# A fused attention and two-MoE kernel: result tiles stored one batch at a time, and the side work of the first expert respread

## The chip, the cores and the metric

The kernel runs on 1 core of one Trainium2 chip. The metric is device time in microseconds (us) of one execution. Before the change it is 998.13 us (median of 3 runs, 998.01 to 1000.34). Engines are called as in the profile: PE is TensorE (PEld its weight loads), DVE VectorE, ACT ScalarE, POOL GpSimd, SP the engine that issues the transfers.

## The reference, cut to what matters

```python
x = attention(q, k, v)              # 4 x 8 heads, 576 rows of 64, window 128 -> x: 2304 x 512
x = moe(x, phi, w1, w2)             # soft slots; its result is c @ slot_out, 32 slots

def _moe2_ref(x, w_gate, w1, w2):   # N = 2304, D = 512, E = 8, F = 1024
    logits = x @ w_gate
    logits = logits - logits.max()
    P = np.exp(logits)
    for _ in range(8):
        P /= P.sum(1, keepdims=True) + 1e-09
        P /= P.sum(0, keepdims=True) + 1e-09
        P *= N / E
    out = np.zeros((N, D))
    for e in range(E):
        h = np.maximum(x @ w1[e], 0.0)
        out += P[:, e:e + 1] * (h @ w2[e])
    return out
```

The change touches the second MoE only: the eight normalising rounds on P, the preparation of an expert's weights, and the store of `out`.

## The kernel before, in words

**Stages.** Attention comes first; the first MoE's own products (L775, L849) run from 165.5 to 202.4 us of the span, and from the first `emit_z` at 210.9 us to the end the second MoE does its eight experts. The rest is about this last stage.

**The main loop.** The 2304 rows are 18 tiles of 128 rows; tile t holds 64 rows of batch 2bp and the same 64 rows of batch 2bp + 1, with `bp, c = divmod(t, 9)`. The loop is over m = 0 to 71, and m is expert e = m // 9 and n = m % 9: one m does the two tiles n and n + 9. The hidden layer h is made by `emit_z` (L967, twice for one m, 4 matmuls each) from the factored first MoE (`ct`) and the expert's `stk`; the second product is a Strassen-like scheme of 7 block products, each of 12 matmuls in halves of f16 (`prod`, L1039). So one m has 7 steps k_ = 0 to 6, and in step k_ the program issues, in this order: `emit_z` (k_ 0 and 1, for m + 1), `step` (the product of the step on PE and the `add` of an earlier product to `acc`), at k_ = 0 also `last(m - 1)` and `left(m, 7)`, then **one step of the side work** (`next(side, None)`), then `left(m + 1, k_)`, which makes one piece of the next m's left operands: on ACT (L977, L988, L996), DVE (L980, L992) and POOL (L999). The order within an engine is the order of the program; every engine works through its own list in order and waits where an operand is missing.

**The adds.** In the first expert (e = 0) the first add of a block is a copy on ACT (L1049), the others are adds on DVE (L1051); from e = 1 on all are DVE operations that multiply by the gate's column `pe_[e]` (L1053). PE overwrites a product's PSUM buffer only when the add has read it.

**The side work** is a chain of generators, each `yield` one step. For the next expert: `prep_w1` (32 matmuls L676, a maximum, scales, the copy of `stk`), a load of weights, `prep_w2a` and another load. `prep_w2a` first takes the magnitudes of the second weight matrix, 8 passes on ACT (L564), then their maximum, a power-of-two scale, and then in 44 steps turns the matrix into the seven f16 block operands `w2h` and `w2l`: casts on ACT (L637), scalings on ACT (L645), differences on POOL (L634). In the first expert there is more: `gate` (logits and exp of P) comes first in 6 steps, then `sinkhorn`, the eight rounds on P, stepped together with the preparation of expert 1 by `par`, one step of each for each step of the loop. A round has three steps: (A) five DVE operations L923 to L928 on P, (B) a matmul L930 that sums over partitions, (C) four DVE operations L933 to L936. What is left of the side work at n = 8, k_ = 2 is issued there in one go ("the drain").

**The stores.** In the last expert a tile is complete after its last add, and `store` (L1060 to L1064) issues one transfer for it on SP's queue: 128 rows of 512 f32, 256 KB, as 2 batches x 64 rows x 512; the very last tiles go in two halves of columns.

Of the kernel before, what the change touches and what calls it, by code (L numbers as in the profile page):

```python
# [12 lines left out]
ALU = mybir.AluOpType  # L13
# [11 lines left out]
def tile_kernel(ctx: ExitStack, tc: tile.TileContext, q, k, v, phi, w1, w2, w_gate, m1, m2, rel, out):  # L25
    nc = tc.nc
    B, H, S, D = q.shape
    N, DM = out.shape
    E, _, F = w1.shape
    NS = phi.shape[1]  # L30
    CH = 64
# [63 lines left out]
    with tc.manual_schedule():  # L95
        with ExitStack() as ab:
# [5 lines left out]
            with ExitStack() as at:  # L102
# [369 lines left out]
                side = []  # L472
# [12 lines left out]
                s = 0  # L485
                while s < NST + 4 or side or px:
                    t, hf = divmod(s, 2)
# [28 lines left out]
                    if s < NST and hf == 0:  # L516
                        bp, c = divmod(t, NCH)
# [27 lines left out]
            stk = {}  # L545
            w2c = {}
            wsum = {}

            def spread(am):

                dg = mp.tile([128, 128], F32, tag="sl", name="dg", bufs=1)
                nc.vector.tensor_scalar_mul(dg, idn, am)
                return dg
# [1 line left out]
            def largest(dg, ps):  # L555
                nc.tensor.matmul(ps, lhsT=ones, rhs=dg, start=True, stop=True)

            def prep_w2a(e, place):
                wsum[e] = mp.tile([128, 4, 256], F32, tag="t1", name="t1", bufs=1)

                am = mp.tile([128, 1], F32, tag="am2", name="am2")
                amp = mp.tile([128, FC], F32, tag="amp", name="amp")
                for i in range(FC):
                    nc.scalar.activation(out=wsum[e][:, 0:2].rearrange("p a b -> p (a b)"),  # L564
                                         in_=wt["m2", e][:, DM * i:DM * (i + 1)], func=AF.Abs, accum_out=amp[:, i:i + 1])
                    yield
                yield
                nc.vector.tensor_reduce(out=am, in_=amp, axis=AX.X, op=ALU.max)
                dg = spread(am)
                yield  # L570
                ps = place()
                largest(dg, ps)
# [146 lines left out]
            with ExitStack() as bs:  # L719
# [75 lines left out]
                for i in range(4):  # L795
                    for cp in range(4):
                        dst = selh if cp < 2 else sell
                        nc.vector.tensor_copy(out=dst[32 * i:32 * i + 32, 32 * cp:32 * cp + 32],
                                              in_=idn[32 * i:32 * i + 32, 32 * i:32 * i + 32])
# [79 lines left out]
            with ExitStack() as ms:  # L879
                ap_ = ms.enter_context(tc.tile_pool(name="acc", bufs=1, reuse_waits="tile"))  # L880
                acc = ap_.tile([128, NT, DM], F32, name="acc")
# [7 lines left out]
                def gate():  # L889

                    st4 = sp.tile([128, DC, 4, NS], F32, name="st4")
                    sgb = sp.tile([128, 4, E], F32, name="sgb")
                    nc.gpsimd.memset(sgb, 0.0)
                    nc.vector.tensor_copy(out=st4, in_=st.unsqueeze(2).to_broadcast([128, DC, 4, NS]))
                    yield
                    ps = pmt
                    for dc in range(DC):
                        nc.tensor.matmul(ps[:, 0:E], lhsT=st4[:, dc].rearrange("p a b -> p (a b)"),
                                         rhs=wg_sb[:, dc, :], start=(dc == 0), stop=(dc == DC - 1))
                    for i in range(4):  # L900
                        nc.scalar.copy(out=sgb[32 * i:32 * i + 32, i, :], in_=ps[32 * i:32 * i + 32, 0:E])
                    yield
                    yield
                    for g in range(NG):
                        nc.tensor.matmul(ps[:, 32 * g:32 * g + 32], lhsT=cTf[:, g, :],
                                         rhs=sgb.rearrange("p a b -> p (a b)"), start=True, stop=True)
                    l2 = ps[:, 0:NT * E]
                    mx = mp.tile([128, 1], F32, tag="mx", name="mx")
                    mg = mp.tile([128, 1], F32, tag="mg", name="mg")
                    nc.vector.tensor_reduce(out=mx, in_=l2, axis=AX.X, op=ALU.max)  # L910
                    dg = spread(mx)
                    yield
                    largest(dg, ps[:, 256:384])
                    yield
                    nc.vector.tensor_reduce(out=mg, in_=ps[:, 256:384], axis=AX.X, op=ALU.max, negate=True)
                    nc.scalar.activation(out=prob.rearrange("p a b -> p (a b)"), in_=l2, func=AF.Exp, bias=mg)
                    yield

                def sinkhorn():
                    sums_ = pmt[:, 384:384 + E]  # L920
                    for _ in range(8):
                        rs_ = mp.tile([128, NT], F32, tag="rs", name="rs")
                        nc.vector.tensor_reduce(out=rs_, in_=prob, axis=AX.X, op=ALU.add)  # L923
                        nc.vector.tensor_scalar_add(rs_, rs_, 1e-9)
                        nc.vector.reciprocal(rs_, rs_)
                        nc.vector.tensor_tensor(out=prob, in0=prob, in1=rs_.to_broadcast([128, NT, E]), op=ALU.mult)
                        c1 = mp.tile([128, E], F32, tag="c1", name="c1")
                        nc.vector.tensor_reduce(out=c1, in_=prob.rearrange("p t e -> p e t"), axis=AX.X, op=ALU.add)  # L928
                        yield
                        nc.tensor.matmul(sums_, lhsT=ones, rhs=c1, start=True, stop=True)  # L930
                        yield
                        c2 = mp.tile([128, E], F32, tag="c2", name="c2")
                        nc.vector.tensor_scalar_add(c2, sums_, 1e-9)  # L933
                        nc.vector.reciprocal(c2, c2)
                        nc.vector.tensor_scalar_mul(c2, c2, float(N) / E)
                        nc.vector.tensor_tensor(out=prob, in0=prob,  # L936
                                                in1=c2.unsqueeze(1).to_broadcast([128, NT, E]), op=ALU.mult)
                        yield
# [3 lines left out]
                def scale_p(e):  # L942
                    pe_[e] = mp.tile([128, NT], F32, tag="pe", name="pe", bufs=3)
                    nc.vector.tensor_scalar(out=pe_[e], in0=prob[:, :, e], scalar1=inv_s[:, e:e + 1],
                                            scalar2=inv_w[:, e:e + 1], op0=ALU.mult, op1=ALU.mult)
                    yield
# [4 lines left out]
                NP = NT // 2  # L951
# [107 lines left out]

                def store(t, c0=0, c1=DM):  # L1060
                    bp, c = divmod(t, NCH)
                    nc.sync.dma_start(
                        out=out.rearrange("(b s) d -> b s d", s=S)[2 * bp:2 * bp + 2, CH * c:CH * c + CH, c0:c1],
                        in_=acc[:, t, c0:c1])  # L1064

                NM = E * NP

# [44 lines left out]
                def chain(*gens):  # L1112
                    for g_ in gens:
                        yield from g_

                def par(x_, y_):

                    live = [x_, y_]
                    while live:
                        for g_ in list(live):  # L1120
                            if next(g_, 0) == 0:
                                live.remove(g_)
                        yield

                def loads(e, nm):
# [26 lines left out]
                for m in range(NM):  # L1152
                    e, n = divmod(m, NP)
                    if n == 0:
                        side = []
                        if e + 1 < E:
                            side = [prep_w1(e + 1), loads(e + 2, "m1"), prep_w2a(e + 1, lambda: pmt[:, 256:384]), loads(e + 2, "m2")]
                        if e == 0:
                            side = [gate(), par(chain(sinkhorn(), scale_p(0)), chain(*side))]
                        if e + 1 < E:  # L1160
                            side.append(scale_p(e + 1))
                        side = chain(*side)
                    for k_ in range(7):
                        if m and k_ < 2 and m + 1 < NM:
                            emit_z(m + 1, k_)
                        if m or k_ > 3:
                            step(m, k_)
                        elif k_ == 0:

                            step(m, 0)  # L1170
                            emit_z(m + 1, 0)
                            step(m, 1)
                            step(m, 2)
                        elif k_ == 1:
                            emit_z(m + 1, 1)
                            for kk_, nm in ((KS1, "s1"), (KS4, "s4")):
                                hi_s(0, kk_, nm)
                                lo_s(0, kk_, nm)
                            step(m, 3)
                        if k_ == 0:  # L1180
                            if m:
                                last(m - 1)
                            left(m, 7)
                        next(side, None)
                        if k_ in (4, 5) and NP - 1 <= m < 2 * NP - 1:
                            weigh((m + 1) % NP + NP * (k_ - 4))
                        if m + 1 < NM:
                            left(m + 1, k_)
                        if n == NP - 1 and k_ == 2:
                            for _ in side:  # L1190
                                pass
                last(NM - 1)
# [37 lines left out]
```

## Time and profile before

| | before |
|---|---|
| median of 3 runs | 998.13 us |
| profiled execution: its time | 1000.32 us |
| profiled execution: its span (first to last instruction) | 998.5 us |
| PE busy | 954.0 us, 96% |
| DVE busy | 746.4 us, 75% |
| ACT busy | 625.3 us, 63% |
| POOL busy | 574.9 us, 58% |
| mean granted clock of PE | 0.985 |

How to read it: the span is that of the profiled execution; its time has 1.8 us more around it. Busy time is an average over stages with different limits, so the shares of the whole span don't tell what bounds one stage; the rows below are therefore taken by stretches. A granted clock of 1.00 is 2.4 GHz, 0.50 is 1.2 GHz. A busy PE is not PE at its peak, as matmuls are pipelined.

### The profile page before, as it was taken

How to read it: one execution, taken by the hardware profiler on the slowest of the kernel's cores; microseconds unless marked ns; L12 is line 12 of the kernel's file. 1: busy time of each engine (PE TensorE's matmuls, PEld its weight loads, DVE VectorE, ACT ScalarE, POOL GpSimd, SP SyncE). 2: the span in 40 equal slices, each digit the busy share in tenths (PEclk: the TensorE clock that was granted, in tenths of full speed). 3: DMA queues.
4: the chain of work that ended last, by engine and by line, in shares of the span. 5: the costliest groups of instructions: out<-in, count | busy, mean ns of one | idle time of the engine just before them, and what ended most of it. 6: DMA issues, size and time to landing. Idle time of an engine off the chain costs nothing.

```text
span 998.5 us, 24140 instructions
## 1 busy us (share of the span) xinstructions
PE 954.0 (96%) x9341; PEld 815.9 (82%) x9341; DVE 746.4 (75%) x1932; ACT 625.3 (63%) x1529; POOL 574.9 (58%) x685
## 2 busy tenths in 40 slices
PE   8999999888899899999999999999999999999993
PEld 7887886356778788888888888888888888888883
DVE  6888895768965587777778777777787777777771
ACT  6878884734667577756656664766566656564540
POOL 2322211213389568947884896589569947884440
PEclk9999999999999999999999999999999999999997
DMA  8999998950200220041022002200220020001111
GB/s 180 251 237 215 249 278 297 386 200 13 84 1 1 94 88 1 2 136 46 2 80 101 2 2 88 93 2 2 94 88 1 2 95 2 2 1 40 53 52 48
DMA packets 93927, 90.07 MB, mean 90 GB/s; under 512 B 63094, under 2 KB 67062, under 8 KB 93814
## 3 DMA queue, kind: packets, MB, share of 16 engines
q1 hardware_dynamic: 93814, 88.54, 29.6%
q8 instruction: 73, 1.20, 0.5%
q14 instruction: 40, 0.33, 0.1%
HBM read 81.97 MB, written 4.72 MB: 87 GB/s over the span
## 4 chain that ended last, share of the span: by engine, by line
PE 85%; DVE 10%; ACT 2%; issue 1%; POOL 1%; DVEq 0%; POOLq 0%; ACTq 0%
PE x L1039 36%; PE y L1039 26%; PE z L967 6%; PE xp L276 4%; PE s L202 3%; PE pt L251 2%; PE pt L155 2%; PE m L676 2%; PE b L775 1%; DVE et L221 1%; DVE et L240 1%; DVE ops L980 1%; PE s L849 1%; PE pt L290 1%; PE warm L83 1%
## 5 line engine op out<-in xcount | busy, mean ns | idle before, releaser
L1039 PEld LDWEIGHTS <-ops 128*128 128x128 f16 x6048 | 595.1, 98 | 82.4 <-issue 9.8
L999 POOL TENSOR_TENSOR ops<-s,ops 128x512 f16<-128x512 f32 x287 | 331.7, 1159 | 236.2 <-ACT ops L996 198.7
L1039 PE MATMUL x<-w2h,ops 128*128 128x256 f16 x2304 | 418.5, 275 | 7.1 <-ACT acc L1049 3.2
L1039 PE MATMUL y<-w2h,ops 128*128 128x256 f16 x1728 | 319.5, 273 | 1.6 <-DVE acc L1051 1.6
L1039 PE MATMUL x<-w2l,ops 128*128 128x256 f16 x1152 | 316.4, 275 | 0.0
L996 ACT CAST ops<-s 128x512 f16<-128x512 f32 x288 | 177.7, 618 | 213.3 <-DVE s L992 210.9
L1039 PE MATMUL y<-w2l,ops 128*128 128x256 f16 x864 | 235.6, 273 | 0.0
L1053 DVE SCALAR_TENSOR_TENSOR acc<-x,pe,acc 128x256 f32<-128x256 f32 x252 | 121.7, 483 | 74.9 <-PE x L1039 71.0
L977 ACT ACTIVATE ops<-z 128x512 f16<-128x512 f32 x216 | 128.5, 595 | 37.5 <-PE z L967 34.7
L980 DVE SCALAR_TENSOR_TENSOR ops<-z,ops 128x512 f16<-128x512 f32 x216 | 147.1, 681 | 0.0
L1053 DVE SCALAR_TENSOR_TENSOR acc<-y,pe,acc 128x256 f32<-128x256 f32 x189 | 91.4, 483 | 60.8 <-PE y L1039 59.1
L634 POOL TENSOR_TENSOR w2l<-w,w2h 128x256 f16<-128x256 f32 x168 | 112.1, 673 | 0.0
L992 DVE SCALAR_TENSOR_TENSOR s<-z,r 128x512 f32<-128x512 f32 x144 | 98.2, 682 | 9.2 <-ACT r L988 4.4
L992 DVE SCALAR_TENSOR_TENSOR s<-z,s 128x512 f32<-128x512 f32 x144 | 98.0, 681 | 0.0
L181 POOL TENSOR_SCALAR qn<-qn 128x128 f32<-128x128 f32 x64 | 35.0, 555 | 99.1 <-DMA qn<-in_q_dram 80.0
L967 PE MATMUL z<-ct,stk 128*128 128x256 f16 x576 | 87.4, 275 | 3.0 <-DVE ops L980 2.2
L637 ACT CAST w2h<-w 128x256 f16<-128x256 f32 x168 | 66.3, 402 | 4.3 <-POOL w L634 4.2
L967 PEld LDWEIGHTS <-stk 128*128 128x128 f16 x576 | 55.9, 99 | 13.2 <-issue 3.1
L230 ACT ACTIVATE et<-et,mx 128x192 f32<-128x192 f32 (+2 forms) x144 | 61.2, 434 | 1.2 <-DVE mx L221 1.1
L202 PE MATMUL s<-kT,qT 128*128 128x192 f32 (+2 forms) x288 | 50.2, 317 | 0.1
L221 DVE CUSTOM_DVE_ANT_0 et<-s,rel_sb 128x192 f32<-128x192 f32 (+2 forms) x144 | 40.2, 326 | 8.5 <-PE s L202 8.1
L202 PEld LDWEIGHTS s<-kT,qT 128*128 128x128 f32 x288 | 43.7, 191 | 3.4 <-issue 3.4
(197 smaller groups left out, 949.2 us busy)
## 6 DMA issues: line engine op xcount, KB each, us to landing
w<-in_moe_w_dram SPq DMA_DIRECT2D x68, 512.0 KB
w<-in_moe_w_dram SPq DMA_DIRECT2D x14, 2048.0 KB
kn<-in_k_dram SPq DMA_DIRECT2D x36, 128.0 KB
qn<-in_q_dram SPq DMA_DIRECT2D x36, 128.0 KB
v<-in_v_dram SPq DMA_DIRECT2D x18, 256.0 KB
out_dram<-acc SPq DMA_DIRECT2D x17, 256.0 KB
w<-in_moe_w_dram SPq DMA_DIRECT2D x2, 1024.0 KB
stk<-sh SPq DMA_DIRECT2D x56, 16.0 KB
```

Of the source, the lines that this page charges most:

```text
L202: nc.tensor.matmul(ps[gg][:, j, col:192], lhsT=qT[:, g, j, :], rhs=kT[:, g, j, k0:k1], start=True, stop=True)
L230: nc.scalar.activation(out=runs[hh], in_=runs[hh], func=AF.Exp, bias=mx[:, hh:hh + 1], scale=-1.0, accum_out=sm[:, hh:hh + 1])
L634: nc.gpsimd.tensor_tensor(out=out_, in0=x_, in1=y_, op=ALU.subtract)
L637: nc.scalar.copy(out=hi[:, i, r], in_=src[:, r])
L967: nc.tensor.matmul(ps[:, i], lhsT=stk[e][:, 128 * ft:128 * ft + 128], rhs=ct.rearrange("p (a n) t -> p a n t", a=2)[:, :, n, :], start=Tru ...
L977: nc.scalar.activation(out=ops_[m][:, k_, 0], in_=zb(m, i, j), func=AF.Relu)
L980: nc.vector.scalar_tensor_tensor(out=ops_[m][:, k_, 1], in0=zb(m, i, j), scalar=0.0, in1=ops_[m][:, k_, 0], op0=ALU.max, op1=ALU.subtract)
L992: nc.vector.scalar_tensor_tensor(out=new_sum(m, nm), in0=zb(m, i, j), scalar=0.0, in1=o, op0=ALU.max, op1=op)
L996: nc.scalar.copy(out=ops_[m][:, k_, 0], in_=sm_[m, nm])
L999: eng.tensor_tensor(out=ops_[m][:, k_, 1], in0=sm_[m, nm], in1=ops_[m][:, k_, 0], op=ALU.subtract)
L1039: nc.tensor.matmul(out_, lhsT=a_[:, k_, l_, i, :], rhs=r_[:, k_, i, :], start=(first and j == 0), stop=(j == 11), skip_group_check=True)
L1053: nc.vector.scalar_tensor_tensor(out=o, in0=ps, scalar=pe_[e][:, t:t + 1], in1=o, op0=ALU.mult, op1=ALU.add)
```

## The change

1. **The store.** One tile is stored by two transfers, each the 64 rows of one batch (64 x 512 f32, 128 KB) instead of one of 2 x 64 x 512. 38 transfers are issued instead of 19; the bytes are the same.
2. **The rounds.** The first step of `sinkhorn` is no longer followed by one with each step of the loop: `par` gets a flag, and with it the rounds rest in every third step while the preparation of the next expert goes on. 24 steps of rounds take 36 steps of the loop.
3. **The magnitudes.** The 8 passes on ACT become a generator of their own, `magnitude`. In the first expert they run beside `gate` (`par(gate(), magnitude(1))`), ahead of the rounds; in the others they stay where they were.
4. **The column scale.** The two DVE operations L933 and L935 become one with two constants: 1 / ((s + 1e-9) E / N) instead of (1 / (s + 1e-9)) N / E.
5. **The drain** moves from k_ = 2 to k_ = 4 of n = 8, in every expert.

```diff
+            def magnitude(e):
                 wsum[e] = mp.tile([128, 4, 256], F32, tag="t1", name="t1", bufs=1)
...
                 nc.vector.tensor_reduce(out=am, in_=amp, axis=AX.X, op=ALU.max)
-                dg = spread(am)
+                bound[e] = am
+
+            def prep_w2a(e, place):
+                if e not in bound:
+                    yield from magnitude(e)
+                dg = spread(bound.pop(e))
...
-                        nc.vector.tensor_scalar_add(c2, sums_, 1e-9)
+                        nc.vector.tensor_scalar(out=c2, in0=sums_, scalar1=1e-9, scalar2=float(E) / N,
+                                                op0=ALU.add, op1=ALU.mult)
                         nc.vector.reciprocal(c2, c2)
-                        nc.vector.tensor_scalar_mul(c2, c2, float(N) / E)
...
-                    nc.sync.dma_start(
-                        out=out.rearrange("(b s) d -> b s d", s=S)[2 * bp:2 * bp + 2, CH * c:CH * c + CH, c0:c1],
-                        in_=acc[:, t, c0:c1])
+                    for j in range(2):
+                        r0 = S * (2 * bp + j) + CH * c
+                        nc.sync.dma_start(out=out[r0:r0 + CH, c0:c1], in_=acc[CH * j:CH * j + CH, t, c0:c1])
...
+                            if rests and g_ is x_ and i % 3 == 2 and len(live) > 1:
+                                continue
...
-                            side = [gate(), par(chain(sinkhorn(), scale_p(0)), chain(*side))]
+                            side = [par(gate(), magnitude(1)),
+                                    par(chain(sinkhorn(), scale_p(0)), chain(*side), True)]
...
-                        if n == NP - 1 and k_ == 2:
+                        if n == NP - 1 and k_ == 4:
                             for _ in side:
                                 pass
```

**On ACT, beside the gate** (m = 0 of the loop, from the copy of the gate's weights `sgb` on; L996 and L977 make the operands of m = 1, L1049 are the copies of products, `prob` is P). Before:

```order
L901 COPY sgb<-m 32x8 x4
L977 ACTIVATE ops<-z 128x512
L996 CAST ops<-s_3679 128x512
L977 ACTIVATE ops<-z 128x512
L996 CAST ops<-s_3696 128x512
L996 CAST ops<-s_3714 128x512
L1049 COPY acc<-x 128x256
L916 ACTIVATE prob<-m,mg 128x144
L1049 COPY acc<-x 128x256
```

and in the changed kernel:

```order
L907 COPY sgb<-m 32x8 x4
L565 ACTIVATE t_3646,amp<-w 128x512
L983 ACTIVATE ops<-z 128x512
L565 ACTIVATE t_3646,amp<-w 128x512
L1002 CAST ops<-s_3684 128x512
L983 ACTIVATE ops<-z 128x512
L565 ACTIVATE t_3646,amp<-w 128x512
L1002 CAST ops<-s_3703 128x512
L565 ACTIVATE t_3646,amp<-w 128x512
L1002 CAST ops<-s_3722 128x512
L1055 COPY acc<-x 128x256
L922 ACTIVATE prob<-m,mg 128x144
```

Passes of the magnitudes (L565) now stand between the casts and copies that PE waits for; four of the eight are seen here.

**On DVE, in the rounds** (one step C and the step A after it, or what now lies between; L980 and L992 make left operands, L1051 is an add of a product). Before:

```order
L992 SCALAR_TENSOR_TENSOR s_3968<-z,s_3898 128x512
L1051 TENSOR_TENSOR acc<-y,acc 128x256
L980 SCALAR_TENSOR_TENSOR ops<-z,ops 128x512
L933 TENSOR_SCALAR c_3993<-m 128x8
L934 RECIPROCAL c_3993<-c_3993 128x8
L935 TENSOR_SCALAR c_3993<-c_3993 128x8
L936 TENSOR_TENSOR prob<-prob,c_3993 128x144
L923 TENSOR_REDUCE rs<-prob 128x18
L924 TENSOR_SCALAR rs<-rs 128x18
L925 RECIPROCAL rs<-rs 128x18
L926 TENSOR_TENSOR prob<-prob,rs 128x144
L928 TENSOR_REDUCE c_4025<-prob 128x8
```

and in the changed kernel:

```order
L986 SCALAR_TENSOR_TENSOR ops<-z,ops 128x512
L939 TENSOR_SCALAR c_4167<-m 128x8
L941 RECIPROCAL c_4167<-c_4167 128x8
L942 TENSOR_TENSOR prob<-prob,c_4167 128x144
L998 SCALAR_TENSOR_TENSOR s_4172<-z,r_4147 128x512
L1057 TENSOR_TENSOR acc<-y,acc 128x256
L929 TENSOR_REDUCE rs<-prob 128x18
L930 TENSOR_SCALAR rs<-rs 128x18
L931 RECIPROCAL rs<-rs 128x18
L932 TENSOR_TENSOR prob<-prob,rs 128x144
```

Step C is one operation shorter, and operations of the main loop stand more often between the steps of a round.

**On ACT, at the end of the first expert** (n = 8; L637 are casts of the next expert's weights, L1058 scales a finished tile by its gate column). Before, and then in the changed kernel:

```order
L977 ACTIVATE ops<-z 128x512
L637 CAST w2h<-w 128x256 x3
L637 CAST w2h<-t_3922 128x256
L637 CAST w2h<-w 128x256 x2
L1049 COPY acc<-x 128x256
L996 CAST ops<-s_4991 128x512
```

```order
L983 ACTIVATE ops<-z 128x512
L1055 COPY acc<-x 128x256
L643 CAST w2h<-t_3646 128x256
L1002 CAST ops<-s_4974 128x512
L643 CAST w2h<-w 128x256
L1064 ACTIVATE acc<-acc,pe 128x512
L1002 CAST ops<-s_4994 128x512
L643 CAST w2h<-w 128x256
L1055 COPY acc<-x 128x256
```

The drain's six casts in a row ahead of the copy of a product are gone; single casts stand between the loop's operations.

## Rows read from the trace of the kernel before

**Rows 1.** Busy time by stretch: us, busy us (instructions) by engine, PEclk, DMA share, GB/s.

```profile
217.00:230.60 13.60, 12.80 (x102) 10.87 (x99) 9.49 (x19) 7.62 (x19) 5.88 (x5) 0.87 0.01 3
230.60:281.50 50.90, 42.81 (x365) 34.45 (x365) 45.15 (x120) 27.64 (x66) 19.91 (x21) 0.95 0.13 48
281.50:325.00 43.50, 43.27 (x390) 38.35 (x389) 24.98 (x44) 32.45 (x75) 38.91 (x48) 0.98 0.01 2
325.00:335.00 10.00, 7.29 (x56) 5.79 (x59) 3.72 (x7) 6.04 (x13) 7.84 (x11) 0.83 0.44 139
335.00:428.50 93.50, 92.98 (x868) 82.33 (x872) 71.66 (x143) 68.20 (x141) 69.69 (x81) 1.00 0.14 47
...
903.50:997.50 94.00, 78.88 (x723) 70.44 (x720) 57.50 (x107) 33.17 (x57) 33.52 (x29) 0.94 0.14 51
```

**Rows 2.** The transfers of the store line L1062: duration of an issue in ns, first and last.

```profile
L1062 SPq DMA_DIRECT2D out_dram<-acc x19: 511/512/4930, 902.1 to 983.8; - x19
```

**Rows 3.** Timeline, the last add before the end: start us, us, engine, line.

```profile
982.41 0.48 DVE L1053 SCALAR_TENSOR_TENSOR acc<-y,pe,acc 128x256 f32<-128x256 f32 x1 [0.82 <-PE y L1039]
```

**Rows 4.** Busy time by stretch: a load of weights, and the end of the stores.

```profile
250.00:255.00 5.00, 5.00 (x38) 4.07 (x37) 4.31 (x13) 4.57 (x12) 1.65 (x2) 0.78 0.95 383
...
997.00:998.00 1.00, 0.00 (x0) 0.00 (x0) 0.00 (x0) 0.00 (x0) 0.00 (x0) 0.50 0.03 11
```

**Rows 5.** Timeline, the first loads (two of 64 x 8 x 64 f32, 128 KB each) and their first use.

```profile
0.73 1.44 SPq L129 DMA_DIRECT2D kn<-in_k_dram  x2
...
5.05 1.09 PE L155 MATMUL pt<-idn,kn 128*128 128x128 f32 x4
```

**Rows 6.** Waits of PE from 217 to 335 us: us in total, times, longest.

```profile
PE m L930 <- DVE c L928: 3.9, 5, 2.0
PE x L1039 <- ACT acc L1049: 3.2, 2, 2.9
PE z L967 <- DVE ops L980: 2.2, 2, 1.1
PE y L1039 <- DVE acc L1051: 1.6, 2, 0.8
PE m L905 <- ACT sgb L901: 0.8, 1, 0.8
```

**Rows 7.** Groups on DVE from 230 to 280 us: busy us, mean ns, idle before.

```profile
L926 DVE TENSOR_TENSOR prob<-prob,rs 128x144 f32<-128x144 f32 x8 | 4.9, 609 | 0.3
...
L936 DVE TENSOR_TENSOR prob<-prob,c 128x144 f32<-128x144 f32 x8 | 4.2, 529 | 0.3
...
L935 DVE TENSOR_SCALAR c<-c 128x8 f32<-128x8 f32 x8 | 4.1, 509 | 0.3
...
L924 DVE TENSOR_SCALAR rs<-rs 128x18 f32<-128x18 f32 x7 | 2.0, 289 | 0.2
```

**Rows 8.** Timeline in the rounds: one line of DVE beside POOL, and alone.

```profile
245.69 1.15 POOL L999 TENSOR_TENSOR ops<-s,ops 128x512 f16<-128x512 f32 x1 [1.49 <-ACT ops L996]
245.71 1.29 DVE L926 TENSOR_TENSOR prob<-prob,rs 128x144 f32<-128x144 f32 x1
...
251.78 0.31 DVE L926 TENSOR_TENSOR prob<-prob,rs 128x144 f32<-128x144 f32 x1
```

**Rows 9.** Groups on ACT from 216 to 330 us: a pass of the magnitudes.

```profile
L564 ACT ACTIVATE t<-w 128x512 f32<-128x512 f32 x8 | 5.1, 634 | 0.0
...
L564 ACT ACTIVATION_READ_ACCUMULATOR t<-w 128x1 f32 x8 | 1.6, 195 | 0.0
```

**Rows 10.** Groups on PE from 217 to 335 us: the rounds' column sums.

```profile
L930 PE MATMUL m<-c,ones 128*128 128x8 f32 x16 | 2.9, 254 | 4.0 <-DVE c L928 3.9
```

**Rows 11.** The chain that ended last, in order of time: start us, us, what.

```profile
283.29 1.31 PE y L1039 x12
...
964.47 0.44 PE z L967 x4
```

**Rows 12.** Busy time by stretch: the end of the loads of expert 1's weights.

```profile
217.50:218.00 0.50, 0.50 (x7) 0.44 (x6) 0.49 (x1) 0.50 (x2) 0.00 (x0) 1.00 0.07 25
```

More of the change, by code (lines that the diff above doesn't have):

```diff
@@ L547, in tile_kernel @@
             wsum = {}
+            bound = {}
             def spread(am):
@@ L556, in largest @@
                 nc.tensor.matmul(ps, lhsT=ones, rhs=dg, start=True, stop=True)
-            def prep_w2a(e, place):
+            def magnitude(e):
                 wsum[e] = mp.tile([128, 4, 256], F32, tag="t1", name="t1", bufs=1)
@@ L1114, in chain, with par @@
                         yield from g_
-                def par(x_, y_):
-                    live = [x_, y_]
+                def par(x_, y_, rests=False):
+                    live, i = [x_, y_], 0
                     while live:
                         for g_ in list(live):
+                            if rests and g_ is x_ and i % 3 == 2 and len(live) > 1:
+                                continue
                             if next(g_, 0) == 0:
                                 live.remove(g_)
+                        i += 1
                         yield
```

## The prediction

> **What bounds the kernel now.** I read first the busy times by stretch. In a later expert PE works 92.98 of 93.50 us at a granted clock of 1.00 [rows 1]: nothing is to be had there. Two places differ. In the first expert, 217.0 to 335.0 us (118.0 us), PE is busy 12.80 + 42.81 + 43.27 + 7.29 = 106.2 us, so 11.8 us are idle, and the granted clock falls: 1 less the clock, times the length of each of the four stretches, is 1.8 + 2.5 + 0.9 + 1.7 = 6.9 us lost to the slow level [rows 1]. Together 18.7 us. And behind the last add, which ends at 982.41 + 0.48 = 982.9 us [rows 3], the span goes on for 15.6 us to 998.5.
>
> **The end** is the stores. The first is issued at 902.1 us [rows 2], and from 903.5 to 997.5 the queue moves 51 GB/s with a DMA share of 0.14, which is 2 of 16 engines always busy, where a load of weights takes 0.95 and moves 383 GB/s [rows 1, 4]. 18 tiles in 94 us are 5.2 us for each. PE makes two tiles in one m, 7 x 1.31 + 2 x 0.44 = 10.05 us [rows 11], 5.0 us each. So the stores are a little slower than the products, and what is left queues up behind the last add.
>
> **The first expert.** The waits of PE name DVE (the column sum L930 waits for step A's L928, `emit_z` for L980, a product for L1051: 3.9 + 2.2 + 1.6 us) and ACT (3.2 us, all but 0.3 of it one wait of 2.9 at the drain; 0.8 us at the gate) [rows 6]. From 230.6 to 281.5 us, where the 24 steps of the rounds run, DVE is busy 45.15 of 50.9 us. PE would need for them 24 x 10.05 / 7 = 34.5 us, 2.9 for the sums [rows 10] and at most 93.5 - 9 x 10.05 = 3.1 for the preparation's matmuls: 40.5. DVE needs more than PE there, so PE must wait, and after waits its clock falls. From 281.5 to 325 DVE is busy only 57% and PE hardly idle [rows 1].
>
> **The store, priced.** The last tile goes out in two issues of 0.51 us [rows 2], 982.9 + 1.0 = 983.9. What a store of 64 rows needs from its issue to its landing no row shows. The nearest are the first loads, 64 rows and 128 KB each: the second issue ends at 0.73 + 1.44 = 2.17 and both are used at 5.05 [rows 5], so at most 2.9 us; from below I put nothing. Behind the last byte (11 of some 50 GB/s in the last us, so about 997.2) the span has 1.3 us more [rows 4]. The end lies between 983.9 + 1.3 = 985.2 and 988.1; I take 986.8, near the middle, since the last pieces are half as large as those loads. Gain 998.5 - 986.8 = **11.7 us**, bounds 10.4 and 13.3. The 19 issues more cost SP 1.0 us for a tile against 5.0, and SP waits for tiles anyway. The Trainium skill, "DMA: Bandwidth & Descriptors", section "Why a DMA increments its semaphore by 16 and not by 1", says that a transfer runs on the largest number of engines up to 16 that divides the slowest dimension of both sides: 2 for 2 x 64 x 512, 16 for 64 rows. With the share of 0.14 the trace agrees for the 2; no store here shows the 16.
>
> **The rounds, priced.** A usual step costs DVE 24.98 / 43.5 x 10.05 / 7 = 0.82 us [rows 1, 11]. Of the 45.15 us, 24 x 0.82 = 19.7 are usual work and 25.4 the rounds with the preparation's small scales. The fused scale takes out L935, 4.1 us in all, long for 8 values [rows 7]. The rounds then take 36 steps: DVE 25.4 - 4.1 + 36 x 0.82 = 50.8 us, PE 36 x 10.05 / 7 + 2.9 + 3.1 = 57.7. DVE is no longer the slower one, at 88%. But it works in bursts (step A, five operations, is still followed by a matmul of PE one or two steps later), and something speaks against the move: the conversions of expert 1 now begin some 5 steps earlier, while the rounds last to about step 47 of 63, so some 6 of 8 rounds run beside a POOL that is busy 38.91 of 43.5 us, 89%, instead of 19.91 of 50.9, 39% [rows 1]. L926 takes 0.31 us alone, 1.29 where a POOL operation runs from 245.69 to 246.84; it ends right behind that [rows 8]. Its mean is 0.30 over this; if 0.2 for L936 and 0.1 for L924 are of the same kind [rows 7], a round waits 0.6 us now and, in proportion to POOL's share, 1.4 then: 8 x 0.8 = 6.5 us more at most, DVE 57.3, level with PE. The Trainium skill, "SBUF — State Buffer", section "SBUF: two separate sides", calls this an exclusive lock, which a VectorE operation with two SBUF inputs and a GpSimd operation hold for a whole instruction. The row agrees; by it the move costs something like the 6.5, without it nothing.
>
> Now the rounds lose 8.1 us idle and 2.5 of clock [rows 1]. Between nothing (but for 1 us of bursts) and the present 10.6 I take 4: DVE at 88 to 99%, some short waits and one fall of the clock.
>
> **The gate, priced.** The 8 passes of the magnitudes, 0.634 + 0.195 us each [rows 9], are 6.6 us that move between ACT's casts and copies. ACT is busy 7.62 of 13.6 us there [rows 1], so it gets about full, and the copies that free PE's buffers stand behind them. Against that, `prep_w1`'s matmuls leave this place for the rounds (they are in the 3.1 above), so PE may wait that long for nothing. The first pass also waits for its weights, whose load ends by 218.0 [rows 12], half a us at most. I leave the present loss there (0.8 idle, 1.8 clock) and add 0.8; bounds 0 and 3.
>
> **The drain, priced.** Six casts in a row, behind POOL's differences, hold up the copy for which PE waits 2.9 us [rows 6], and the clock is 0.83 in that stretch, 1.7 us [rows 1]. With single casts between the loop's operations I expect 0.5 of it left; from e = 1 on, where PE loses 0.5 us in a whole expert [rows 1], the move of the drain is worth nothing. What would come late next is the last f16 block, which PE needs only in the next m. The rest of the 18.7 is the 0.9 of clock from 281.5 on and 0.2 idle; it belongs to the rounds' last wait and goes or stays with them, I leave 0.3.
>
> **Sum.** The first expert loses 2.6 + 0.8 + 4 + 0.5 + 0.3 = 8.2 instead of 18.7: gain **10.5 us**, bounds 5 (gate 3, rounds 7.5) and 15. With 11.7: **22.2 us**. From the profiled execution's own 1000.32 us that gives 978.1. The median of the runs, 998.13, is 2.2 lower, and the same sum from it gives **976.0**, which I predict. The bounds are 998.1 - 28 = 970 and 998.1 - 15.4 = 982.7.
>
> **Rivals.**
> *A, the rounds gain nothing:* POOL and DVE block each other in every round, POOL falls behind, and DVE and POOL together set the pace as DVE does now. For: 89% and 1.29 us [rows 1, 8]. Against: the same POOL load runs without a wait of PE from 281.5 on, and L935 is gone. Then only the drain and the end gain, about 4 + 11.7: 982.4.
> *B, the stores are no faster:* writing, not the spread over engines, sets 51 GB/s, and two halves take as long as one whole. The change then does not do what it says. Against: 14 of 16 engines idle. The stores start and end 10.5 us earlier: 987.6.
> *C, slower:* each store, now one unbroken block of 128 KB in the output, goes to a single engine. At 25 GB/s the 4.72 MB need 188 us from about 893: 1081. It decides from the point where a tile's store takes longer than PE's 5.0 us, so below 52 GB/s; the kernel already stands on that edge with 51. Against: the loads of 64 rows come from many separate pieces and do spread [rows 5], which says little of a block.
>
> **How the numbers follow.** Forecast 0.75, A 0.15, B 0.06, C 0.04. The range 970 to 983.5 takes in the forecast's bounds and A's centre; B and C are left out, with some of A and of the forecast's edges, about 2 in 10. Within 0.3% (3 us, about what a measurement of this kernel can tell from no change) nothing lies but mixtures of failures: 0.01. Faster 0.95, slower 0.04.
>
> **What would show it.** Right: the last byte lands within 5 us of the last add, and the DMA share in the last expert is short peaks instead of 0.14 throughout; the first expert lasts some 107 us instead of 118; no wait of PE over 2 us for an ACT copy at the drain; L926 and L936 (with new line numbers) have longer means than 609 and 529 ns. Wrong: a share of 0.14 or 0.07 to the end (B, C); DVE busy over 95% in the rounds with waits of PE for the column sum as now (A); waits of PE for ACT's copies in m = 0 and 1 beyond 3 us.

## The result, and the profile after

The changed kernel takes **984.23 us** (median of 4 runs, 983.94 to 984.86); in the same comparison the kernel before took 999.24 us (998.01 to 1000.93). The ratio is 0.985, 95% interval 0.9831 to 0.9868: faster by 15 us, 1.5%, clear of the scatter. Forecast were 976.0 us and a range of 970 to 983.5, so the sign was right, and the gain about two thirds of the 22.2 us.

| profiled execution, us | before | after |
|---|---|---|
| its time / its span | 1000.32 / 998.5 | 984.86 / 983.1 |
| first expert (from the loop's first `emit_z`, in m = 0, to `prep_w1` of expert 2) | 117.9 | 112.3 |
| from there to the end of the last add | 648.0 | 648.0 |
| behind the last add | 15.6 | 5.1 |
| mean granted clock of PE | 0.985 | 0.992 |

The seven later experts are the same to 0.1 us. So there are two places to read, as before.

**The first expert.** Busy time by stretch in the changed kernel, to set against [rows 1] (us, busy us of PE, PEld, DVE, ACT, POOL, PEclk, DMA share, GB/s):

```profile
217.70:231.80 14.10, 13.11 (x103) 10.91 (x102) 7.49 (x15) 11.20 (x32) 5.72 (x5) 0.88 0.02 8
231.80:249.50 17.70, 16.89 (x170) 14.05 (x168) 12.41 (x34) 9.40 (x22) 5.76 (x5) 1.00 0.04 9
249.50:260.00 10.50, 4.40 (x25) 3.16 (x23) 3.89 (x14) 1.38 (x3) 1.16 (x1) 0.67 0.41 131
260.00:301.50 41.50, 39.17 (x356) 34.01 (x355) 37.62 (x83) 29.15 (x68) 33.76 (x40) 1.00 0.06 22
301.50:330.00 28.50, 28.50 (x263) 25.42 (x262) 19.06 (x35) 21.68 (x49) 26.38 (x32) 1.00 0.01 2
```

The clock is full in all lines but two: 0.88 in the first, beside the gate, which was 0.87 before, and 0.67 in the third. In the third line, 10.5 us, PE works 4.4 us, **and so do all the others less**: DVE 3.9, ACT 1.4, POOL 1.2. When all engines stand still together, it is worth asking whether one of them is held by something that is not an engine. The waits of PE and of DVE there, from 205 and 217 to 340 us, name it (who <- for whom: us in total, times, longest):

```profile
PE m L557 <- DVE dg L553: 6.8, 2, 6.0
PE z L973 <- DVE ops L986: 2.5, 2, 1.6
PE m L911 <- ACT sgb L907: 0.8, 1, 0.8
PE m L936 <- DVE c L934: 0.6, 1, 0.6
...
DVE dg L553 <- DMA stk<-sl: 7.0, 1, 7.0
```

The waits of [rows 6] have become small: for the column sums 0.6 instead of 3.9, for the copy at the drain none. In their place stands one that was not there: PE waits 6.0 us for `dg`, and DVE waited 7.0 us before `dg` for a **DMA**. The timeline of the changed kernel around it (start us, us, engine, line; SPq is SP's queue of transfers):

```profile
243.62 6.01 SPq L710 DMA_DIRECT2D stk<-sh  x8
248.57 0.41 DVE L934 TENSOR_REDUCE c<-prob 128x8 f32<-128x144 f32 x1
249.73 4.97 SPq L710 DMA_DIRECT2D stk<-sl  x8
254.80 0.53 SPq L64 DMA_DIRECT2D w<-in_moe_w_dram  x1
255.94 0.29 DVE L553 TENSOR_SCALAR dg<-idn,am 128x128 f32<-128x128 f32 x1 [6.96 <-DMA stk<-sl]
256.28 0.80 PE L557 MATMUL m<-dg,ones 128*128 128x128 f32 x2 [5.97 <-DVE dg L553]
```

`dg`, the diagonal from which a matmul spreads a maximum over the partitions, is `spread`'s tile with the tag `"sl"` and one buffer. `sl` of `prep_w1` has the same tag: it is the source of the second half of the 16 transfers that build `stk`. So `dg` may be written only when the last of them has read `sl`. SP issues all 16 one after another, the last at 254.1 us; it lands 1.8 us later, at 255.9, and `dg` is written at 255.94. DVE, which works in order, holds everything behind it meanwhile. In the kernel before the same pair of lines read

```profile
242.68 4.97 SPq L704 DMA_DIRECT2D stk<-sl  x8
...
261.55 0.29 DVE L552 TENSOR_SCALAR dg<-idn,am 128x128 f32<-128x128 f32 x1
```

with the eight passes of the magnitudes between them: 13.9 us, in which the transfers were long done. The magnitudes went to the gate, and with them the cover. Behind the standstill the product at 257.2 us takes 2.72 instead of 1.31 us, at the slow clock.

**The end.** The changed kernel's last add, the issues on SP, and the stretches behind (as [rows 2 to 4]):

```profile
L1070 SPq DMA_DIRECT2D out_dram<-acc x38: 466/594/1545, 897.3 to 979.8; - x38
...
976.75 3.66 SPq L1070 DMA_DIRECT2D out_dram<-acc  x6
...
977.55 0.48 DVE L1059 SCALAR_TENSOR_TENSOR acc<-y,pe,acc 128x256 f32<-128x256 f32 x1 [0.82 <-PE y L1045]
...
978.00:979.00 1.00, 0.00 (x0) 0.00 (x0) 0.03 (x1) 0.00 (x0) 0.00 (x0) 1.00 0.95 203
979.00:980.00 1.00, 0.00 (x0) 0.00 (x0) 0.00 (x0) 0.00 (x0) 0.00 (x0) 1.00 0.60 137
980.00:981.00 1.00, 0.00 (x0) 0.00 (x0) 0.00 (x0) 0.00 (x0) 0.00 (x0) 0.55 0.40 88
981.00:982.00 1.00, 0.00 (x0) 0.00 (x0) 0.00 (x0) 0.00 (x0) 0.00 (x0) 0.50 0.29 66
```

The DMA share reaches 0.95, where it stood at 0.14. The last add ends at 978.0 us; the last of the six issues that come together starts at 979.8, since each takes 0.6 us, and the median landing is 2.0 us after the issue for the small stores and 2.4 for the large.

### The profile page after: what moved, and what is told of

Same layout as the page of the kernel before. It is cut to its first block, busy times and chain, and to the rows that moved or that the text cites. A ratio compares the mean times of both kernels' runs of the same rounds, so it can differ in the third digit from the quotient of the medians.

```text
span 983.1 us, 24146 instructions
## 1 busy us (share of the span) xinstructions
PE 950.5 (97%) x9341; PEld 814.4 (83%) x9341; DVE 744.9 (76%) x1924; ACT 624.4 (64%) x1529; POOL 574.3 (58%) x685
## 4 chain that ended last, share of the span: by engine, by line
PE 67%; DVE 2%; ACT 0%; issue 0%
PE x L1045 34%; PE y L1045 26%; PE z L973 6%; PE m L682 1%; DVE acc L1059 1%; DVE ops L986 0%; DVE sl L702 0%; ACT sh L701 0%; PE m L557 0%; DVE ar L696 0%; DVE w1i L92 0%; DVE w1p L91 0%; DVE w1p L90 0%; DVE acc L1057 0%; PE m L936 0%
```

## The experiments

All times are medians; ratios are against the kernel before on the same chip, with their 95% interval. As the kernel before itself took 998.5 to 1001.1 us in these comparisons, runs of different comparisons are set beside each other by the lengths of their stretches, which the last table gives.

**1. `dg` in a place of its own.** The changed kernel; `dg` goes to a part of the magnitudes' scratch that lies idle then.

```diff
-            def spread(am):
+            def spread(am, dg=None):
-                dg = mp.tile([128, 128], F32, tag="sl", name="dg", bufs=1)
+                if dg is None:
+                    dg = mp.tile([128, 128], F32, tag="sl", name="dg", bufs=1)
...
-                dg = spread(bound.pop(e))
+                dg = spread(bound.pop(e), wsum[e][:, 2, 0:128])
```

> The changed kernel, but the diagonal for expert maxima of w2 (dg) is written to an unused part of the magnitudes' scratch instead of the one buffer that it shares with sl, the source of the stk transfers. Theory 1 (DVE stands still for 7.0 us because dg must wait until the transfers stk<-sl have read that buffer, PE for 6.0 us behind it, and the clock falls for another 1.4): the wait is gone, the first expert is 7.4 us shorter, about 976.8 us. Theory 2 (DVE with POOL's locks is the bound of the rounds, and the standstill only takes time that other waits would take): the waits of PE for the column sums and for emit_z grow instead, 981 us or more. Theory 3 (the wait is for the transfers' time in SP's queue and moves to the next user of the buffer): about 984.

Measured: 977.85 us, ratio 0.9793 (0.9775 to 0.9811). The first expert takes 104.7 us instead of 112.3. The waits of PE from 205 to 340 us:

```profile
PE z L974 <- DVE ops L987: 2.4, 2, 1.6
PE m L937 <- DVE c L935: 1.4, 2, 0.8
PE m L558 <- DVE dg L554: 0.9, 1, 0.9
```

The standstill is gone and no other wait takes its place; the others grow by less than 1 us. Theory 1 holds; theories 2 and 3 fall.

**2 and 3. The two halves of the change alone.** First the kernel before with only the new store, then the changed kernel with only the old store.

```diff
-                    nc.sync.dma_start(
-                        out=out.rearrange("(b s) d -> b s d", s=S)[2 * bp:2 * bp + 2, CH * c:CH * c + CH, c0:c1],
-                        in_=acc[:, t, c0:c1])
+                    for j in range(2):
+                        r0 = S * (2 * bp + j) + CH * c
+                        nc.sync.dma_start(out=out[r0:r0 + CH, c0:c1], in_=acc[CH * j:CH * j + CH, t, c0:c1])
```

> The kernel before with the new store alone. From the two traces the span behind the last add shrinks from 15.6 to 5.1 us: 10.5 us, about 988 us, DMA share in short peaks. If the end gained only because the products ended earlier or later, it would stay above 993.

Measured: 988.41 us, ratio 0.9893 (0.9876 to 0.9910). Behind the last add 4.8 us.

> The changed kernel with the old store. The first expert is 5.6 us shorter, but the stores move 51 GB/s from the first one on, so the end comes 94 us after the first store plus some: about 993.5 us. If the two parts were not additive (the old store hidden behind a later start) it would be below 990.

Measured: 995.37 us, ratio 0.9962 (0.9948 to 0.9976). Behind the last add 15.7 us.

The halves add up: 0.9893 x 0.9962 = 0.9855, and both together measured 0.985. So the store gave 10 us of the gain, and the first expert only some 3 to 4. Run 3 ends 2 us later than expected: the 5.6 us that I gave the first expert were the difference of two profiled executions, and the one before was not a short one (see below).

**4. The magnitudes beside the gate, without the rests and with the old drain.**

```diff
-                                    par(chain(sinkhorn(), scale_p(0)), chain(*side), True)]
+                                    par(chain(sinkhorn(), scale_p(0)), chain(*side))]
...
-                        if n == NP - 1 and k_ == 4:
+                        if n == NP - 1 and k_ == 2:
```

> The changed kernel with the rounds in every step and the drain at k_ = 2 as before, so that of the first expert's changes the magnitudes beside the gate and the fused scale are left. Theory 1: dg comes as soon behind the stk transfers as in the changed kernel, the wait for DMA on DVE is there again (5 to 8 us), and the rounds keep the losses of before: about 990 us, slower than the store alone. Theory 2: the standstill belongs to the spacing of the rounds and is not there: about 986.

Measured: 987.56 us, ratio 0.9886 (0.9871 to 0.9902): between the two forecasts, and not to be told from the store alone. Waits of DVE and PE:

```profile
DVE dg L553 <- DMA stk<-sl: 6.3, 1, 6.3
...
PE m L557 <- DVE dg L553: 3.6, 2, 2.8
PE z L973 <- DVE ops L986: 2.8, 3, 1.1
PE m L936 <- DVE c L934: 1.9, 3, 0.9
```

The wait for the transfers is there, so it comes with the magnitudes' move and not with the rests, as theory 1 says. But only 2.8 us of it at a time reach PE, and the time I had named for theory 1 was too long. The trace shows what covers the rest: when DVE stops, at 250.5 us, PE is behind it and still has two products to do, until 254.3 us; it had just waited 0.9 and 1.1 us for DVE, and the first of the two products takes 2.72 us.

**5 to 7. The other parts, one by one, with `dg` in its own place.** Each is run 1 with one part of the change undone.

```diff
-                                    par(chain(sinkhorn(), scale_p(0)), chain(*side), True)]
+                                    par(chain(sinkhorn(), scale_p(0)), chain(*side))]
```

> The run with dg in its own place (977.85 us), but the rounds in every step of the loop as before. By the prediction's sum DVE then needs 45.2 - 4.1 = 41.1 us for 24 steps and PE 40.5, and DVE works in bursts: the waits of PE for DVE in the rounds come back, 4 to 8 us, about 983. If the rests do nothing now that dg waits for no transfer and L935 is gone: 978.

Measured: 981.29 us, ratio 0.9804 (0.9788 to 0.9820); first expert 108.1 us. Waits of PE from 215 to 340 us:

```profile
PE m L937 <- DVE c L935: 3.2, 5, 1.1
PE z L974 <- DVE ops L987: 2.8, 3, 1.1
PE x L1046 <- ACT acc L1056: 1.0, 1, 1.0
```

The rests are worth 3.4 us, less than the 4 to 8 expected. The wait for the column sums comes back, with 1.8 us more than in run 1. The wait for ACT's copy is not of the rests: it stands at 231.4 us, beside the gate, and runs 6 and 7, which rest, have it too.

```diff
-                        nc.vector.tensor_scalar(out=c2, in0=sums_, scalar1=1e-9, scalar2=float(E) / N,
-                                                op0=ALU.add, op1=ALU.mult)
+                        nc.vector.tensor_scalar_add(c2, sums_, 1e-9)
                         nc.vector.reciprocal(c2, c2)
+                        nc.vector.tensor_scalar_mul(c2, c2, float(N) / E)
```

> The run with dg in its own place, but the column scale in three operations again. DVE gets 4 us more in the rounds (8 x 0.5), which at 88% has room for it: if DVE is no longer the bound, 978 to 979. If POOL's locks have brought it level with PE, all of it shows: 981 to 982.

Measured: 979.30 us, ratio 0.9785 (0.9770 to 0.9801); first expert 106.0 us. The fused scale is worth some 1.3 us of the 4.1 that L935 was busy, little more than the scatter (977.5 to 980.2 us in run 1, 978.9 to 980.3 here): for most of that time DVE is no longer the bound.

```diff
-                        if n == NP - 1 and k_ == 4:
+                        if n == NP - 1 and k_ == 2:
```

> The run with dg in its own place, but the drain at k_ = 2 of n = 8. The magnitudes beside the gate end the side work some 9 steps earlier, so little is left to drain: if that is what took the 2.9 us wait away, 978; if the later place of the drain did, the wait for the copy is back, and with the clock 981 to 982.

Measured: 977.90 us, ratio 0.9771 (0.9754 to 0.9788); first expert 104.4 us. The place of the drain is worth nothing that these runs can tell. Three casts stand in a row there, from 314.5 to 315.5 us, where the kernel before has six, and PE waits for no copy behind them: what took the 2.9 us wait away is that less side work is left by then.

**8. Two queues at the end.** Run 1, and in the last m the second batch's half of each store on ACT's queue.

```diff
-                def store(t, c0=0, c1=DM):
+                def store(t, c0=0, c1=DM, two=False):
...
-                        nc.sync.dma_start(out=out[r0:r0 + CH, c0:c1], in_=acc[CH * j:CH * j + CH, t, c0:c1])
+                        (nc.scalar if two and j else nc.sync).dma_start(out=out[r0:r0 + CH, c0:c1], in_=acc[CH * j:CH * j + CH, t, c0:c1])
...
-                            store(n + NP)
+                            store(n + NP, two=m == NM - 1)
...
-                            store(n, 0, 256)
+                            store(n, 0, 256, two=True)
...
-                        store(n, 256)
+                        store(n, 256, two=True)
```

> The run with dg in its own place; in the last m the second batch's half of each store is issued on ACT's queue instead of SP's. In the changed kernel SP issues the last six transfers one after another, 3.66 us, so that the last starts 1.8 us behind the last add. If this queue at the end is what made it 5.1 instead of the predicted 3.9 us, the span ends 1.0 to 1.5 us earlier: about 976.7. If the landing alone sets it: 977.8.

Measured: **976.27 us** (976.06 to 976.40), ratio 0.9754 (0.9739 to 0.9770). SP's and ACT's issues, the last add (timeline), and the stretches behind it:

```profile
969.17 1.78 SPq L1071 DMA_DIRECT2D out_dram<-acc  x3
969.18 2.04 ACTq L1071 DMA_DIRECT2D out_dram<-acc  x3
...
969.97 0.48 DVE L1060 SCALAR_TENSOR_TENSOR acc<-y,pe,acc 128x256 f32<-128x256 f32 x1 [0.82 <-PE y L1046]
...
971.00:972.00 1.00, 0.00 (x0) 0.00 (x0) 0.00 (x0) 0.00 (x0) 0.00 (x0) 1.00 0.88 290
972.00:973.00 1.00, 0.00 (x0) 0.00 (x0) 0.00 (x0) 0.00 (x0) 0.00 (x0) 1.00 0.35 99
```

Behind the last add 3.9 us, where run 1 has 5.1: SP's queue held the end by 1.2 us. This kernel is faster than the kernel before and than the changed one.

**9. As many transfers, but cut by columns.** The kernel before.

```diff
-                    nc.sync.dma_start(
-                        out=out.rearrange("(b s) d -> b s d", s=S)[2 * bp:2 * bp + 2, CH * c:CH * c + CH, c0:c1],
-                        in_=acc[:, t, c0:c1])
+                    h = (c1 - c0) // 2
+                    for a in (c0, c0 + h):
+                        nc.sync.dma_start(
+                            out=out.rearrange("(b s) d -> b s d", s=S)[2 * bp:2 * bp + 2, CH * c:CH * c + CH, a:a + h],
+                            in_=acc[:, t, a:a + h])
```

> The kernel before, each store cut into two transfers by columns (2 x 64 x 256 each) instead of by batch: as many transfers and bytes for each as in the change, but the outer dimension stays 2. If the spread over engines is what the new store gains: no gain, DMA share still 0.14 and some 50 GB/s to the end, 15 to 16 us behind the last add, about 998 us. If it is the number of transfers in flight or their size: an end as in the changed kernel, about 988.

Measured: 1006.01 us, ratio 1.0054 (1.0034 to 1.0074), half a per cent **slower**. Stretches of the store, first in the kernel before:

```profile
905.00:975.00 70.00, 70.00 (x643) 62.74 (x642) 52.69 (x99) 32.30 (x56) 32.12 (x28) 1.00 0.14 52
983.00:997.00 14.00, 0.00 (x0) 0.00 (x0) 0.00 (x0) 0.00 (x0) 0.00 (x0) 0.61 0.13 50
```

and in this run, with its last one:

```profile
905.00:975.00 70.00, 70.00 (x644) 62.74 (x642) 52.79 (x98) 30.42 (x53) 32.46 (x28) 1.00 0.14 50
983.00:997.00 14.00, 0.00 (x0) 0.00 (x0) 0.00 (x0) 0.00 (x0) 0.00 (x0) 0.54 0.14 47
...
999.00:1000.00 1.00, 0.00 (x0) 0.00 (x0) 0.00 (x0) 0.00 (x0) 0.00 (x0) 0.50 0.14 44
```

The share stays 0.14, and the rate falls a little, from 52 and 50 to 50 and 47 GB/s. So the number and size of the transfers give nothing; it is the cut by batch, with an outer dimension of 64 rows instead of 2 batches, that gives the 10 us. One thing more differs here: the rows written are 1 KB long instead of 2 KB. The trace of the changed kernel speaks against that as the reason. Its last four stores are cut by columns as well, 64 rows x 256 in pieces of 1 KB that do not join, and from 981 to 982 us, when the 66 KB of the last of them move alone, the share is 0.29 over the whole us, which is 4.6 of 16 engines.

**10. More rest.** Run 8, with the rounds resting in every second step.

```diff
-                            if rests and g_ is x_ and i % 3 == 2 and len(live) > 1:
+                            if rests and g_ is x_ and i % 2 == 1 and len(live) > 1:
```

> The run with two queues at the end (976.27 us), but the rounds rest in every second step instead of every third: 24 steps take 48 of the loop. DVE's demand in the rounds falls to 25.4 - 4.1 + 48 x 0.82 = 60.7 us against PE's 48 x 1.436 + 6 = 74.9, 81%. If the 3.8 us of waits for L935 and L987 that are left are bursts of DVE: about 2 us less, 974. If they are single coincidences: no change, 976; if the later end of the rounds meets the drain: 977 to 978.

Measured: 975.98 us, ratio 0.9759 (0.9743 to 0.9775): not to be told from run 8. The wait for the column sums is gone, but one for ACT's copies is there instead; for `emit_z` PE waits as before:

```profile
PE z L974 <- DVE ops L987: 2.4, 2, 1.5
PE x L1046 <- ACT acc L1056: 1.5, 2, 1.0
PE m L912 <- ACT sgb L908: 0.8, 1, 0.8
```

**All stretches together** (profiled executions, us):

| kernel | first expert | to the last add | behind it | median |
|---|---|---|---|---|
| before | 117.9 | 648.0 | 15.6 | 999.24 |
| after | 112.3 | 648.0 | 5.1 | 984.23 |
| 2, new store only | 114.9 | 648.0 | 4.8 | 988.41 |
| 3, old store | 111.9 | 648.0 | 15.7 | 995.37 |
| 4, magnitudes and scale | 115.6 | 648.0 | 4.8 | 987.56 |
| 1, own `dg` | 104.7 | 648.0 | 5.1 | 977.85 |
| 5, 1 without rests | 108.1 | 648.0 | 4.9 | 981.29 |
| 6, 1 with three operations | 106.0 | 648.0 | 5.0 | 979.30 |
| 7, 1 with the early drain | 104.4 | 648.0 | 5.0 | 977.90 |
| 8, 1 with two queues | 105.0 | 648.0 | 3.9 | 976.27 |
| 9, column halves | 114.7 | 648.0 | 21.1 | 1006.01 |
| 10, 8 with more rest | 104.6 | 648.0 | 3.9 | 975.98 |

## Why the prediction was wrong, point by point

**The step that failed** is "The rounds, priced", with "The gate, priced" before it. I followed the moved magnitudes to where they went, ACT beside the gate, and weighed what they would delay there. I did not ask **what they had covered where they stood**: the time between the transfers from `sl` and the next write to the same buffer, by `dg`. The sum had four losses for the first expert and no line for a wait on DMA; that wait cost 112.3 - 104.7 = 7.6 us, shown by run 1. In the profiled executions the forecast missed by 6.8 us (978.1 against 984.86): the 7.6, less 2.7 by which the rest of the first expert came out better than forecast, plus 1.2 at the end, plus 0.7 that the first expert starts later. The median was missed by 8.2, since I had taken 2.2 us off for the distance between the profiled execution and a median of three; the changed kernel's profiled execution lies only 0.6 above its median. It could have been read: the diff moves `dg = spread(...)` itself, `spread` names its tag, and the rows of SP show 16 issues in a row.

**The rest of the first expert** came out a little better than priced. Without that wait it takes 104.7 us, where the sum had 117.9 - 10.5 = 107.4. The rounds: DVE busy 37.6 of 41.5 us in the fourth stretch above, 91%, where 88 to 99% were expected; PE waits 3.8 us for the column sums and `emit_z` in run 1. DVE's waits beside POOL were there, but smaller than the bound. Groups on DVE in the changed kernel, 232 to 302 us, the former L926, L936 and L924:

```profile
L932 DVE TENSOR_TENSOR prob<-prob,rs 128x144 f32<-128x144 f32 x8 | 4.8, 600 | 0.3
L942 DVE TENSOR_TENSOR prob<-prob,c 128x144 f32<-128x144 f32 x7 | 4.5, 647 | 0.2
L930 DVE TENSOR_SCALAR rs<-rs 128x18 f32<-128x18 f32 x8 | 4.3, 539 | 0.3
```

Against [rows 7] the means move by -9, +118 and +250 ns: 0.36 us for a round, 2.9 us in eight rounds, where 6.5 was put as the most. Both L926 and L936 were to have longer means; only L936 has. Rival A is out: with the rests PE waits less (run 5), and without the wait for `dg` the first expert is 13.2 us shorter than before. That its 982.4 us lies nearer to the result than my 976.0 is chance. The gate: from the stretch's first `emit_z` to the first product of m = 1 it was 15.9 us with `prep_w1`'s matmuls (1.9) and is 14.5 without, so 0.5 us more was lost, against 0.8 forecast. The drain: no wait is left, as forecast, and its place matters as little as forecast (run 7).

**The end** was mis-sized: 5.1 us behind the last add instead of 3.9, still above the lower bound of the gain (10.4; it was 10.5). The term that failed is the two issues of 0.51 us, 1.0 us behind the last add: in the changed kernel the last issue ends 2.4 us behind it. Three stores, six transfers of 0.59 us, become ready within 1.3 us of each other, and SP issues them in a row; the sentence that 1.0 us of issuing is little against 5.0 us for a tile holds in the loop, not at its end. Run 8 gives these 1.2 us back. Rivals B and C are out by the share of 0.95, and run 9 shows that it was the spread: whole and cut by columns, stores with an outer dimension of 2 have a share of 0.13 to 0.14. The rule of the Trainium skill, "DMA: Bandwidth & Descriptors", section "Why a DMA increments its semaphore by 16 and not by 1", gives two engines for both forms. The traces agree; that a store of 64 rows takes all 16, as the rule has it, the share of 0.95 allows but does not prove, as several stores are in flight then.

**The profile I argued from** is one execution of a kernel whose executions differ. Over the 31 executions of the kernel before in these comparisons, 997.8 to 1003.1 us, its 1000.32 lies in the middle, so the 2.2 us that I took off for the median of the first three were chance. But runs 2 and 9 have the same first expert, and their profiled executions took 114.9 and 114.7 us for it, not 117.9. (Run 9's is the shortest of its four executions, by 2.7 us.) From 217 to 335 us, first the kernel before, then run 2; the last line is run 2 over the stretch that has a clock of 0.83 in [rows 1]:

```profile
217.00:335.00 118.00, 106.16 (x910) 89.47 (x911) 83.34 (x188) 73.75 (x172) 72.54 (x82) 0.94 0.10 33
```

```profile
217.00:335.00 118.00, 106.17 (x948) 89.98 (x947) 83.81 (x190) 73.81 (x172) 72.56 (x82) 0.97 0.10 34
325.00:335.00 10.00, 7.35 (x84) 5.93 (x83) 3.72 (x7) 5.93 (x13) 7.81 (x10) 1.00 0.44 139
```

As long busy, at a clock of 0.97 instead of 0.94. PE waits the same 2.9 us for the copy at the drain in run 2, but its clock does not fall there. So some 3 us of the 18.7 that I counted as to be had were not lost in every execution; the changed kernel's runs lie within 1 us of each other.

## What to carry to other kernels

When work is moved, list not only what it will delay at its new place but what it covered at the old one: which buffer was reused behind it, and who, a transfer above all, still reads that buffer. One buffer shared by two tiles under one tag is free only as long as the program's order keeps them apart; an in-order engine that has to write it holds everything queued behind the write. And for a transfer, look at its outer dimension before its size: 2 batches outside meant a DMA share of 0.14, some 2 of 16 engines, and halving the transfers so that 64 rows stood outside took 10 us off the end, while halving them the other way made the end 5.5 us longer.

## What the runs showed of the hardware that was not expected

- Issuing is slow enough to be a bound: SP needs 0.59 us for each store of 64 rows and for each small transfer of `stk`, so the 16 of `stk`, begun at 243.6 us, are all issued only at 254.7, and six stores take 3.7 us.
- Cutting the 2-batch stores by columns did not leave the time the same but made the queue slower, from 52 and 50 GB/s to 50 and 47 in the same stretches, at a DMA share of 0.13 to 0.14 in both. Why smaller pieces lose at this share was not tried.
- One program's stage of 115 to 118 us varies by 3 us between executions, while the products after it repeat to 0.1 us. From 217 to 335 us the granted clock was 0.94 in the longest (117.9 us) and 0.97 and 0.99 in runs 2 and 9 (114.9 and 114.7 us). Behind a wait of PE of 2.9 us, the same in all three, the clock of the stretch from 325 us on was 0.83 in the first and 1.00 in the other two.
